# Second-layer router logits: gate matrix as the stationary operand on four column groups, parts added by a 0/1 matrix

## The chip, the cores and the metric

One NeuronCore of one Trainium2 chip runs the whole program. The metric is device time in microseconds (us), from the start to the end of one execution. The profile shows the engines of the core: TensorE (PE for its products, PEld for its weight loads), VectorE (DVE), ScalarE (ACT), GpSimd (POOL) and SyncE (SP, which issues most DMAs).

## The reference, cut to what matters

An attention block gives 2304 rows of 512 numbers. They go through two mixture-of-experts layers with 8 experts each. In both a row goes to the one expert with the largest logit, and the expert's result is scaled by a softmax weight. The change lies in the second layer's router, the line `logits = x @ w_gate`.

```python
def _moe2_ref(x, w_gate, w1, w2):          # x: 2304 x 512, w_gate: 512 x 8
    logits = x @ w_gate
    expert_idx = np.argmax(logits, axis=1)
    logits_shift = logits - logits.max(-1, keepdims=True)
    probs = np.exp(logits_shift)
    probs /= probs.sum(-1, keepdims=True) + 1e-09
    gate_w = probs[np.arange(N), expert_idx]
    out = np.zeros((N, D), dtype=np.float32)
    for e in range(E):
        mask = expert_idx == e
        ...
        xe = x[mask]
        h = np.maximum(xe @ w1[e], 0.0)    # 512 -> 1024
        ye = h @ w2[e]                     # 1024 -> 512
        out[mask] = gate_w[mask, None] * ye
    return out.astype(np.float32)

def reference(**kwargs):
    ...
    x = _moe_ref(x=x, **moe_kwargs)        # first layer
    return _moe2_ref(x=x, **moe2_kwargs)   # second layer
```

## The kernel before

The program has three stretches. Until about 338 us it computes attention and routes the first layer. From there to about 642 us it runs the first layer's experts (L = 0), and after that the second layer's (L = 1). Each layer works in steps of 128 rows that share one expert; `step(L, t)` emits one step.

A step's main work is two products in a split precision: each operand has an upper part (`Wh`, the first of `b.x`, `b.h`) and a lower part (`Wl`, the second of `b.x`, `b.h`), and a product is upper by upper, upper by lower and lower by upper. `s.gemm(0, ph0, ...)` and `s.gemm(0, ph1, ...)` make the two halves of the hidden layer in 12 matmuls each, and `s.gemm(1, py, ...)` makes the result in 24; each matmul streams 512 columns. All are on line L1289.

Around them TensorE transposes in blocks of 128 by 128, four to a call:

- `hT(i, b)` (L1393) transposes half i of the hidden layer, `b.hs[i]`. ScalarE then copies the upper part out of PSUM (`hilo`, L1232), and VectorE subtracts it for the lower part (L1233).
- `xT_pe` (L1228) transposes the gathered rows of the next step into `psx`, again with `hilo` behind it; `next_rows` is both together.
- In the first layer's steps, `yT_pe` (L1334) transposes the last step's result `ysb` into `pm0`, and `yT_ev` (L1337) copies it on ScalarE into `b.hs[0]`, which is free by then.

`logits_pe` (L1330) multiplies this transposed result by the gate matrix `wgT` (128 x 4 x 8, already scaled by -0.5) into `pm1[:, 0:8]`: four float32 products that add up in PSUM, with 128 columns of `b.hs[0]` as weights and 8 columns of `wgT` streaming. `route2` follows on VectorE and ScalarE: minimum (L1350), first index at the minimum (L1351 to L1354, which gives the one-hot `oh`), tanh and the softmax weight (L1356 to L1363). `rank_pe` and `rank_ev` use `oh` two steps later.

The order is written out by hand: an engine does its instructions in the order in which the code emits them. `splits` puts the next expert's weights into upper and lower parts (ScalarE L980, VectorE L983) where an expert changes. The routing of the very last step of layer one is done by `chain1`, a generator that runs beside the second layer's first step; `n1` says how many of its pieces come at each place in that step.

The names: `pm0`, `pm1`, `psx`, `pt0`, `pt1`, `py`, `ph0`, `ph1` are eight PSUM banks of 128 x 512. `pm0` holds nothing but the transposed result in these steps.

Of the kernel before, what the change touches and what calls it, by code (L numbers as in the profile page):

```python
# [8 lines left out]
F32 = mybir.dt.float32  # L9
# [4 lines left out]
ALU = mybir.AluOpType  # L14
# [458 lines left out]
def tile_kernel(ctx, tc, q, k, v, M_prev, z_prev, beta, emb, tau, w1a, w2a, wg, w1b, w2b, out):  # L473
    nc = tc.nc
    B, H, S, D = q.shape
    E, DM, FF = w1a.shape
    NTOK = B * S
    P = 128
    KD, KF = DM // P, FF // P
# [6 lines left out]
    cst = ctx.enter_context(tc.tile_pool(name="cst", bufs=1))  # L486
# [99 lines left out]

    enT = cst.tile([P, KD, E], F32, name="enT")
    wgT = cst.tile([P, KD, E], F32, name="wgT")
    rtau = cst.tile([P, 1], F32, name="rtau")

    def rnorm1(s2, a, hf):
# [17 lines left out]
    def setup_gates(ps_pool, xp):  # L609
        em = xp.tile([E, DM], F32, tag="xb", name="em")  # L610
        sq = rtile([P, 2 * NS * (NS - NE)], "mv", BF16)[0:E, 0:DM]
        sn, sn1 = rtile([E, 1], "sn"), rtile([E, 1], "sn1")

        def load():
            nc.sync.dma_start(out=em, in_=emb)
            nc.sync.dma_start(out=rtau, in_=tau.rearrange("(a b) -> a b", a=1).broadcast_to([P, 1]))
            nc.sync.dma_start(out=wgT, in_=wg.rearrange("(k p) e -> p k e", p=P))

        def squares():
            nc.scalar.activation(out=sq, in_=em, func=AF.Square, accum_out=sn)  # L620
            rnorm1(sn, sn1, half[0:E, 0:1])

        def scale():
            nc.vector.reciprocal(out=rtau, in_=rtau)
            drain(rnorm2(sn, sn, sn1, rtile([E, 1], "sn2")))
            nc.vector.tensor_scalar(out=em, in0=em, scalar1=sn, scalar2=rtau[0:E], op0=ALU.mult, op1=ALU.mult)
            nc.gpsimd.tensor_scalar(out=wgT, in0=wgT, scalar1=-0.5, scalar2=None, op0=ALU.mult)

        def trans():
            ps = setup_gates.ps = ps_pool.tile([P, 512], F32, tag="t", name="psen")  # L630
            for kk in range(KD):
                nc.tensor.transpose(ps[:, E * kk:E * kk + E], em[:, P * kk:P * kk + P], ident[0:E, 0:E])

        def evac():
            nc.vector.tensor_copy(enT.rearrange("p k e -> p (k e)"), setup_gates.ps[:, 0:KD * E])

        return load, squares, scale, trans, evac
# [554 lines left out]
    def rows_of(t):  # L1192

        return xgt[t % 2] if t else xg0
# [19 lines left out]
    psx, pm1, ph1, pt0, pt1, py, pm0, ph0 = (psp.tile([P, 512], F32, name=x) for x in ("psx", "pm1", "ph1", "pt0", "pt1", "py", "pm0", "ph0"))  # L1214
# [11 lines left out]
    def xT_pe(x):  # L1226
        for kk in range(KD):
            nc.tensor.transpose(psx[:, P * kk:P * kk + P], x[:, P * kk:P * kk + P], ident)  # L1228

    def hilo(ps, hl):  # L1230
        hi, lo = hl
        nc.scalar.activation(out=hi, in_=ps, func=AF.Copy)  # L1232
        nc.vector.tensor_tensor(out=lo, in0=ps, in1=hi.bitcast(F32), op=ALU.subtract)  # L1233
# [90 lines left out]
    e2 = []  # L1324
    pts = (pt0, pt1)

    def logits_pe(yT):

        for kk in range(KD):
            nc.tensor.matmul(pm1[:, 0:E], yT[:, P * kk:P * kk + P], wgT[:, kk], start=(kk == 0), stop=(kk == KD - 1))  # L1330

    def yT_pe():
        for kk in range(KD):
            nc.tensor.transpose(pm0[:, P * kk:P * kk + P], ysb[:, P * kk:P * kk + P], ident)  # L1334

    def yT_ev(yT):
        nc.scalar.activation(out=yT, in_=pm0, func=AF.Copy)  # L1337
# [53 lines left out]
    def hT(i, b):  # L1391
        for kk in range(4):
            nc.tensor.transpose(pts[i][:, P * kk:P * kk + P], b.hs[i][:, P * kk:P * kk + P], ident)  # L1393
        hilo(pts[i], b.h[i])

    def next_rows(t):
        xT_pe(rows_of(t))
        hilo(psx, bufs.x)
# [6 lines left out]
    def step(L, t):  # L1405

        s, b = steps[L, t], bufs
        more = 0 < t < NS - 1
        split2 = t > 2
        rt2 = L == 0  # L1410
        late = t >= NT1 - 2
        x = x0 if t == 0 else b.x
        lx = lambda kk: (*x, P * kk)
        lh = lambda kk: (*b.h[kk // 4], P * (kk % 4))
        begin(L, t)
        s.gemm(0, ph0, lx, 0, 0, 3)
        yield
        s.gemm(0, ph0, lx, 0, 3, 9)
        yield
        s.gemm(0, ph0, lx, 0, 9, 12)  # L1420
        if split2:
            s.splits(0, (0, 1))
        nc.scalar.activation(out=b.hs[0], in_=ph0, func=AF.Relu)
        if split2:
            s.splits(1, (0,))

        ahead = (L, t) != (0, NT1 - 1)
        if ahead and split2:
            s.loads(0, (0, 1))
            s.loads(1, (0,))  # L1430
        yield
        s.gemm(0, ph1, lx, 512, 0, 6)
        hT(0, b)
        yield
        rk = L == 0 and 2 <= t <= NT1 - 2
        if rk:
            rank_pe(t - 2)
            rank_ev(t - 2)
        s.gemm(0, ph1, lx, 512, 6, 12)
        last_mm[0] = s.lm[1]  # L1440
        nc.scalar.activation(out=b.hs[1], in_=ph1, func=AF.Relu)
        yield
        if more:
            next_rows(t + 1)
        if rt2:
            yT_pe()
            yT_ev(b.hs[0])
            route2_iov()
        s.gemm(1, py, lh, 0, 0, 3)
        if split2:  # L1450
            s.splits(0, (2,), "h")
        hT(1, b)
        if split2:
            s.splits(0, (2,), "l")
        if more:
            next_step(L, t + 1)
        yield
        s.gemm(1, py, lh, 0, 3, 6)
        cs = (1, 2, 3)
        if t == NE:  # L1460
            s.splits(1, cs)
            cs = ()
        gen = iter(())
        if rt2:
            logits_pe(b.hs[0])
        yield
        s.gemm(1, py, lh, 0, 6, 9)
        if rt2:
            gen = route2(t - 1)
        next(gen, None)  # L1470
        next(gen, None)
        if split2:
            s.splits(0, (3,))
        if split2 and cs:
            s.splits(1, cs)
        if t == 2:
            s.flags()
            s.splits(0, range(4))
            s.loads(0, range(4))
        if not ahead:  # L1480
            e2.append(nc.values_load(ini[0:1, 1, 0:1], engines=[SP_], min_val=0, max_val=E - 1))
            s.loads(0, (0, 1))
            s.loads(1, (0,))
        if split2:
            s.loads(0, (2, 3))
            s.loads(1, (1, 2, 3))
        drain(gen)
        if rk and ((t - 1) % 6 == 0 or t == NT1 - 2):
            c0 = (t - 2) // 6 * 6
            place(c0, t - 1 - c0)  # L1490
        for q_ in range(9, 24, 3):
            yield
            s.gemm(1, py, lh, 0, q_, q_ + 3)
        last_mm[1] = s.lm[1]
        if (L, t) == (1, NT1 - 2):

            nc.gpsimd.drain()
        if rt2:
            nc.gpsimd.dma_start(out=x2[P * (t - 1):P * t, DM:XR], in_=xcb)  # L1499
            if late:  # L1500
                rank_pe(t - 1)
                rank_ev(t - 1)
                place(t - 1, 1)
        if not ahead:

            with tc.If(rg["nt"] <= NT1):
                for c in range(8):
                    for ins in split_chunk(c, rg["wv"]):
                        tc.add_to_no_dep_group("n18", ins)
        end(L, t)  # L1510
# [71 lines left out]
    b = Bufs(lambda i: Wh[0][:, 1, 512 * i:512 * i + 512] if i < 6 else None)  # L1582
# [40 lines left out]
    C = chain0()  # L1623
# [54 lines left out]
    def chain1():  # L1678

        yT_pe()  # L1680
        yT_ev(b.hs[1])
        route2_iov()
        yield
        logits_pe(b.hs[1])
        R = route2(c)
        next(R)
        yield
        next(R)
        yield
        rank_pe(c)  # L1690
        count_pe(pm1[:, 264:264 + E], (c,))
        yield
        next(R)
        rank_ev(c, False)
        yield
        st = {}
        f1 = finish1(1, NS, pm1[:, 264:264 + E], pm1[:, 320:320 + 2 * (NS - NE)], (c,), st)
        for i, x in enumerate(f1):
            next(R, None)
            if i == 3:  # L1700
                drain(R)
                nl = nc.values_load(ini[0:1, 0, 3:4], engines=[SP_], min_val=NT1, max_val=NS)
                nc.sync.dma_start(out=x2[bass.ds((nl - 1) * P, P), DM:XR], in_=xcb)
            yield
            if x == "second":
                second_expert(1)
        gather(1, NE)
        yield
        yield from finish2(1, st)
        fls[1] = st  # L1710

    C, n1 = chain1(), (1, 1, 1, 5, 1, 0, 2, 0, 4, 6, 0)
    s.gemm(0, ph0, lx, 0, 0, 6)
    run(C, n1[0])
    s.gemm(0, ph0, lx, 0, 6, 12)
# [61 lines left out]
```

## Time and profile before

| what | value |
|---|---|
| median of 3 runs | 940.5 us (937.21 to 945.75) |
| the profiled execution | 937.93 us |
| its span, first to last instruction | 936.2 us |
| TensorE products busy | 901.9 us, 96% of the span |
| VectorE, ScalarE, GpSimd busy | 560.7, 525.9 and 278.9 us |

A span is cut by engine: "busy" is time in which an instruction of that engine was under way. Matmuls overlap one another in the pipeline, so the start of one to the start of the next is a better measure of what a matmul costs than its own duration. A group of like instructions in a row is printed as one line with a count.

### The profile page before, as it was taken

The numbers are of one execution on the slowest core, as the hardware profiler recorded it, in microseconds if no ns is written. First come the engines' busy times: TensorE is split into PE (matmuls) and PEld (weight loads), VectorE is DVE, ScalarE is ACT, GpSimd is POOL, SyncE is SP. The second block draws the span as 40 slices with busy tenths as digits, with TensorE's granted clock in tenths as the row PEclk, the third lists the DMA queues.
The fourth block names the chain that finished last, engine by engine and source line by source line (L and its number), as shares of the span: only waits on it lengthen the run. The fifth ranks groups of instructions, "written<-read, shape, count | busy, mean of one in ns | idle before, by whom it ended". The sixth has DMA issues, their size and how long they took to land. (4 is left out here: it accounts for less than half of the span.)

```text
span 936.2 us, 21857 instructions
## 1 busy us (share of the span) xinstructions
PE 901.9 (96%) x5511; PEld 759.0 (81%) x5511; DVE 560.7 (60%) x1825; ACT 525.9 (56%) x1084; POOL 278.9 (30%) x430
## 2 busy tenths in 40 slices
PE   4999999999998999999999999998999999999997
PEld 3888988898887978887788888886868888888885
DVE  4787788787787586548645565543556413473431
ACT  3777868967866754448534563532267424574531
POOL 5555645535542111221221222121112212222221
PEclk9999999999999999999999999999999999999999
DMA  7854748746637116528733405311647613384111
GB/s 159 157 128 90 181 88 238 167 95 136 158 78 241 59 56 224 196 86 279 223 115 102 149 24 168 118 45 39 223 154 266 230 48 119 125 280 161 42 36 38
DMA packets 107562, 129.24 MB, mean 138 GB/s; under 512 B 70906, under 2 KB 70906, under 8 KB 107396
## 3 DMA queue, kind: packets, MB, share of 16 engines
q1 hardware_dynamic: 99364, 104.21, 39.9%
q0 software_dynamic: 8032, 23.22, 7.5%
q8 instruction: 55, 0.90, 0.4%
q14 instruction: 111, 0.91, 0.3%
HBM read 90.32 MB, written 19.25 MB: 117 GB/s over the span
## 5 line engine op out<-in xcount | busy, mean ns | idle before, releaser
L1289 PE MATMUL py<-Wh,b 128*128 (+1 forms) x688 | 243.3, 409 | 2.4 <-DVE b L1233 2.1
L1289 PE MATMUL ph<-Wh,b 128*128 (+1 forms) x672 | 230.5, 403 | 0.9 <-ACTq L1300 0.9
L983 DVE TENSOR_TENSOR Wl<-stg,Wh 128x1024 f32 (+1 forms) x120 | 145.4, 1224 | 87.2 <-ACT Wh L980 74.8
L1289 PEld LDWEIGHTS py<-Wh,b 128*128 128x128 f32 x688 | 129.5, 188 | 30.1 <-DVE b L1233 3.7
L1289 PEld LDWEIGHTS ph<-Wh,b 128*128 128x128 f32 x672 | 126.9, 189 | 30.1 <-ACTq L1300 1.3
L980 ACT ACTIVATE Wh<-stg 128x1024 f32 (+1 forms) x120 | 125.7, 1058 | 24.8 <-DVEq L1300 5.7
L1289 PE MATMUL py<-Wl,b 128*128 (+1 forms) x344 | 135.8, 395 | 0.0
L1289 PE MATMUL ph<-Wl,b 128*128 (+1 forms) x336 | 133.6, 398 | 1.2 <-DVEq L1300 1.2
L1233 DVE TENSOR_TENSOR b<-pt,b 128x512 fp32r<-128x512 f32 x86 | 59.4, 690 | 111.4 <-ACT b L1232 110.3
L355 ACT ACTIVATE att<-psat 128x512 f32<-128x512 f32 (+4 forms) x160 | 69.4, 434 | 59.6 <-PE psat L350 54.2
L370 PE MATMUL psav<-vb,att 128*128 128x128 f32 x640 | 96.0, 281 | 0.5 <-ACT att L355 0.4
L370 PEld LDWEIGHTS psav<-vb,att 128*128 128x128 f32 x640 | 82.7, 191 | 5.9 <-issue 3.8
L1388 POOL DMA_INDIRECT out_dram<-ysb,xca x21 | 26.4, 1258 | 196.4 <-ACTq L1300 126.1
L1232 ACT ACTIVATE b<-pt 128x512 fp32r<-128x512 f32 x86 | 51.5, 598 | 53.7 <-PE pt L1393 40.5
L1383 ACT ACTIVATE ysb<-py,xca 128x512 f32<-128x512 f32 x42 | 28.8, 686 | 87.7 <-PE py L1289 72.4
L337 ACT ACTIVATE a<-a,mx 128x512 f32<-128x512 f32 (+3 forms) x128 | 71.0, 555 | 10.6 <-DVE mx L325 10.3
L325 DVE CUSTOM_DVE_ANT_0 a<-pss,wmask 128x512 f32<-128x512 f32 (+3 forms) x128 | 61.7, 484 | 23.7 <-PE pss L303 23.1
L1289 PEld LDWEIGHTS ph<-Wl,b 128*128 128x128 f32 x336 | 63.7, 190 | 14.9 <-DVEq L1300 1.9
L1289 PEld LDWEIGHTS py<-Wl,b 128*128 128x128 f32 x344 | 65.0, 189 | 10.7
L1198 POOL DMA_INDIRECT xg<-x_scratch,idx x48 | 55.6, 1158 | 38.2 <-POOL xca L1377 10.8
L1499 POOL DMA_DIRECT2D x_scratch<-xcb x21 | 11.9, 565 | 168.9 <-DVE xcb L1363 65.1
L401 POOL TENSOR_TENSOR xb<-tmp,memx 128x256 f32<-128x256 f32 x31 | 22.7, 733 | 125.4 <-DVE tmp L399 125.4
(391 smaller groups left out, 1599.7 us busy)
## 6 DMA issues: line engine op xcount, KB each, us to landing
stg<-in_moe_w_dram SPq DMA_DIRECT2D x120, 512.0 KB
x_scratch<-ysb POOLq DMA_DIRECT2D x22, 256.0 KB, 3.8
L<-L SPq DMA_DIRECT2D x17, 288.0 KB
Hb<-L SPq DMA_DIRECT2D x16, 288.0 KB
H<-H SPq DMA_DIRECT2D x16, 288.0 KB
Hb<-H SPq DMA_DIRECT2D x15, 288.0 KB
qkn<-in_q_dram SPq DMA_DIRECT2D x32, 128.0 KB
qkn<-in_k_dram SPq DMA_DIRECT2D x32, 128.0 KB
```

The lines of the kernel that those rows point to most:

```text
L325: nc.vector.tensor_tensor_reduce(out=av, in0=sv, in1=wv, scale=1.0, scalar=BIG, op0=ALU.add, op1=ALU.min, accum_out=mx[pr],)
L337: nc.scalar.activation(out=a[pr, 0:N], in_=a[pr, 0:N], func=AF.Exp, scale=-1.0, bias=mx[pr], accum_out=rs[pr, c:c + 1])
L355: nc.scalar.activation(out=att[:, 0:N], in_=ps[:, 0:N], func=AF.Copy)
L370: nc.tensor.matmul(ps[:, c], att[:, 128 * kb:128 * kb + 128], vn[:, kb].rearrange("p a d -> p (a d)"), start=(kb == 0), stop=(kb == c))
L980: return nc.scalar.activation(out=chunk(Wh, c, wv), in_=stg[:, c].unsqueeze(1), func=AF.Copy).ins
L983: return nc.vector.tensor_tensor(out=chunk(Wl, c, wv), in0=stg[:, c].unsqueeze(1), in1=chunk(Wh, c, wv).bitcast(F32), op=ALU.subtract).ins
L1198: return nc.gpsimd.indirect_dma_start(out=rows_of(t), out_offset=None, in_=rows, in_offset=bass.IndirectOffsetOnAxis(ap=idx[:, L, t:t + 1] ...
L1232: nc.scalar.activation(out=hi, in_=ps, func=AF.Copy)
L1233: nc.vector.tensor_tensor(out=lo, in0=ps, in1=hi.bitcast(F32), op=ALU.subtract)
L1289: mm = nc.tensor.matmul(ps, x[:, col:col + P], W, start=(first and q_ == qs[0]), stop=(last and q_ == qs[-1]))
L1383: nc.scalar.activation(out=ysb, in_=py, func=AF.Copy, scale=xc[:, 0:1])
L1388: nc.gpsimd.indirect_dma_start(out=out, out_offset=bass.IndirectOffsetOnAxis(ap=xc[:, 1:2].bitcast(I32), axis=0), in_=ysb, in_offset=None, ...
```

## The change

The products of the logits swap sides. The gate matrix, 8 columns for each of the four blocks of 128 inputs, becomes the weights, and the transposed result streams, 128 columns each. Block kk writes partitions 32 kk to 32 kk + 7 of `pm0`, so that each of the four products stands on its own group of 32 columns of the array (`parts_pe`). VectorE copies the 128 x 128 block out (`parts_ev`, over the first 128 columns of `b.hs[0]`, which are no longer needed). A last product with that block as weights and a 128 x 8 matrix `sel` of zeros and ones streaming adds the four parts and turns them into rows by experts (`logits_pe`). `sel` has a one at partition 32 kk + e in column e; the rows of `pm0` between the parts meet zeros.

The transposes of the last result and ScalarE's copy of it move forward, from behind `xT_pe` to right behind `hT(0, b)`. The parts take their old place, ahead of `py`'s first matmuls. VectorE's copy of the parts goes ahead of the lower part of the next rows. In `chain1` there is one more piece, and `n1` is changed by one.

```diff
+    sel = cst.tile([P, E], F32, name="sel")
...
+            nc.gpsimd.memset(sel, 0.0)
+            for kk in range(KD):
+                nc.gpsimd.affine_select(out=sel, in_=sel, pattern=[[-1, E]], compare_op=ALU.not_equal, fill=1.0, base=-32 * kk, channel_multiplier=1)
...
+    def parts_pe(yT):
+        for kk in range(KD):
+            nc.tensor.matmul(pm0[32 * kk:32 * kk + E, 0:P], wgT[:, kk], yT[:, P * kk:P * kk + P], start=True, stop=True)
+
+    def parts_ev(yT):
+        nc.vector.tensor_copy(yT[:, 0:P], pm0[:, 0:P])
+
     def logits_pe(yT):
-        for kk in range(KD):
-            nc.tensor.matmul(pm1[:, 0:E], yT[:, P * kk:P * kk + P], wgT[:, kk], start=(kk == 0), stop=(kk == KD - 1))
+        nc.tensor.matmul(pm1[:, 0:E], yT[:, 0:P], sel, start=True, stop=True)
...
         hT(0, b)
+        if rt2:
+            yT_pe()
+            yT_ev(b.hs[0])
         yield
...
         if more:
-            next_rows(t + 1)
+            xT_pe(rows_of(t + 1))
         if rt2:
-            yT_pe()
-            yT_ev(b.hs[0])
+            parts_pe(b.hs[0])
+            parts_ev(b.hs[0])
+        if more:
+            hilo(psx, b.x)
+        if rt2:
             route2_iov()
...
         route2_iov()
         yield
+        parts_pe(b.hs[1])
+        parts_ev(b.hs[1])
+        yield
         logits_pe(b.hs[1])
...
-    C, n1 = chain1(), (1, 1, 1, 5, 1, 0, 2, 0, 4, 6, 0)
+    C, n1 = chain1(), (1, 1, 1, 6, 1, 0, 2, 0, 4, 6, 0)
```

How this moves instructions is seen best on TensorE in the middle of a first-layer step. Before, from the transposes of the first half of the hidden layer (`hs_5218` is `b.hs[0]`, `pm_5136` is `pm0`, `pm_5131` is `pm1`) to the logits:

```order
L1393 MATMUL pt_5133<-ident,hs_5218 128x128 x4
L1366 LDWEIGHTS tri
...
L1228 MATMUL psx<-ident,xg_5220 128x128 x4
L1334 MATMUL pm_5136<-ident,ysb 128x128 x4
L1289 ISA
L1289 MATMUL py<-Wh_5124,b_5225 128x512
...
L1330 MATMUL pm_5131<-wgT,hs_5218 128x8
L1300 UNCONDITIONAL_BRANCH
L1330 MATMUL pm_5131<-wgT,hs_5218 128x8 x3
```

Now, at the same place (here `hs_5232` is `b.hs[0]`, `pm_5150` is `pm0`, `pm_5145` is `pm1`):

```order
L1406 MATMUL pt_5147<-ident,hs_5232 128x128 x4
L1347 MATMUL pm_5150<-ident,ysb 128x128 x4
L1379 LDWEIGHTS tri
...
L1233 MATMUL psx<-ident,xg_5234 128x128 x4
L1336 MATMUL pm_5150<-hs_5232,wgT 8x128 x4
L1294 ISA
L1294 MATMUL py<-Wh_5138,b_5239 128x512
...
L1343 MATMUL pm_5145<-sel,hs_5232 128x8
```

The four transposes of `ysb` have moved forward past half of a hidden-layer product, the four parts (8 x 128 results) stand where they stood, and one product is left at the place of the logits.

The other place is VectorE in the second layer's first step, where `chain1` routes the last rows. Before (`t8s`, `km_5145` and `oh` are the route's; `b_5226` is the lower part of the transposed hidden half):

```order
L1343 TENSOR_SCALAR iov<-ioer,xcb 128x8
L1350 TENSOR_REDUCE mn<-pm_5131 128x1
L1351 SCALAR_TENSOR_TENSOR t8s<-pm_5131,mn,iov 128x8
L1353 TENSOR_REDUCE km_5145<-t8s 128x1
L1354 TENSOR_SCALAR oh<-t8s,km_5145,xcb 128x8
L1233 TENSOR_TENSOR b_5226<-pt_5133,b_5225 128x512
L1370 SCALAR_TENSOR_TENSOR rj,rkb<-pm_5131,oh 128x8
```

Now (`b_5240` is that lower part):

```order
L1356 TENSOR_SCALAR iov<-ioer,xcb 128x8
L1339 COPY hs_5233<-pm_5150 128x128
L1363 TENSOR_REDUCE mn<-pm_5145 128x1
L1364 SCALAR_TENSOR_TENSOR t8s<-pm_5145,mn,iov 128x8
L1238 TENSOR_TENSOR b_5240<-pt_5147,b_5239 128x512
L1366 TENSOR_REDUCE km_5159<-t8s 128x1
L1367 TENSOR_SCALAR oh<-t8s,km_5159,xcb 128x8
L1383 SCALAR_TENSOR_TENSOR rj,rkb<-pm_5145,oh 128x8
```

The copy of the parts is new, and the two instructions that make `oh` have fallen behind the lower part of the hidden half.

## Rows read from the trace of the kernel before

**Rows 1.** The page's busy times: engine, busy us, share of the span, instructions

```profile
PE 901.9 (96%) x5511; PEld 759.0 (81%) x5511; DVE 560.7 (60%) x1825; ACT 525.9 (56%) x1084; POOL 278.9 (30%) x430
```

**Rows 2.** Busy times in the first layer's stretch; PEclk is the granted clock

```profile
338.00:642.00 304.00, 300.10 (x1613) 247.41 (x1611) 180.29 (x599) 147.60 (x228) 59.15 (x111) 1.00 0.42 136
```

**Rows 3.** What TensorE waited for in that stretch: us, times, longest

```profile
PE py L1289 <- DVE b L1233: 2.1, 2, 1.1
```

**Rows 4.** Timeline of TensorE: the logits of two steps, seven steps apart

```profile
466.28 0.95 PE L1330 MATMUL pm<-wgT,hs 128*128 128x8 f32 x8
...
563.93 0.95 PE L1330 MATMUL pm<-wgT,hs 128*128 128x8 f32 x8
```

**Rows 5.** Groups by form on TensorE: the logits' products

```profile
L1330 PE MATMUL pm<-wgT,hs 128*128 128x8 f32 x176 | 21.0, 245 | 0.0
```

**Rows 6.** Timeline of TensorE in one step: start us, us, operation

```profile
477.54 0.60 PE L1228 MATMUL psx<-ident,xg 128*128 128x128 f32 x4
477.97 0.60 PE L1334 MATMUL pm<-ident,ysb 128*128 128x128 f32 x4
...
480.23 0.95 PE L1330 MATMUL pm<-wgT,hs 128*128 128x8 f32 x8
481.04 0.48 PE L1289 MATMUL py<-Wh,b 128*128 x1
481.36 0.40 PE L1289 MATMUL py<-Wl,b 128*128 x1
481.59 0.63 PE L1289 MATMUL py<-Wh,b 128*128 x2
```

**Rows 7.** Timeline of TensorE in attention, where 64 columns stand between 128

```profile
171.76 0.83 PE L229 MATMUL psm<-mz,pht 128*128 128x130 f32 x6
172.43 1.05 PE L370 MATMUL psav<-vb,att 128*128 128x128 f32 x8
...
173.89 0.38 PE L229 MATMUL psm<-mz,pht 128*128 128x130 f32 x2
174.20 0.43 PE L231 MATMUL psm<-mz,pht 128*64 128x130 f32 x2
174.57 0.94 PE L370 MATMUL psav<-vb,att 128*128 128x128 f32 x6
175.34 0.38 PE L350 MATMUL psat<-ident,a 128*128 128x128 f32 x2
```

**Rows 8.** Timeline of TensorE in attention, ten passes of 64 columns by 64

```profile
103.09 0.80 PE L376 MATMUL psav<-vb,att 128*64 128x64 f32 x10
103.82 0.55 PE L350 MATMUL psat<-ident,a 128*128 128x128 f32 x3
```

**Rows 9.** Timeline of ScalarE in the step of rows 6

```profile
477.73 0.60 ACT L1441 ACTIVATE hs<-ph 128x512 f32<-128x512 f32 x1 [0.94 <-PE ph L1289]
...
478.70 0.61 ACT L1337 ACTIVATE hs<-pm 128x512 f32<-128x512 f32 x1
```

**Rows 10.** Timeline of VectorE in that step

```profile
478.85 0.69 DVE L1233 TENSOR_TENSOR b<-psx,b 128x512 fp32r<-128x512 f32 x1 [1.18 <-ACT b L1232]
```

**Rows 11.** Groups by form on VectorE: a copy out of PSUM

```profile
L220 DVE COPY pht<-pspr 128x64 f32<-128x64 f32 x16 | 3.4, 214 | 0.2
```

**Rows 12.** Groups by form, and timeline, of GpSimd

```profile
L550 POOL TENSOR_SCALAR_AFFINE_SELECT pw<-pw 128x2 f32<-128x2 f32 x12 | 2.3, 189 | 0.5
...
51.95 0.72 POOL L401 TENSOR_TENSOR xb<-tmp,memx 128x256 f32<-128x256 f32 x1 [2.64 <-DVE tmp L399]
```

**Rows 13.** Timeline of VectorE in the second layer's first step

```profile
650.98 0.29 DVE L1354 TENSOR_SCALAR oh<-t8s,km,xcb 128x8 bf16<-128x8 f32 x1
652.81 0.69 DVE L1233 TENSOR_TENSOR b<-pt,b 128x512 fp32r<-128x512 f32 x1 [1.55 <-ACT b L1232]
```

**Rows 14.** Timeline of TensorE in the same place

```profile
653.39 0.18 PE L1366 MATMUL pm<-oh,tri 128*128 128x8 bf16 x1
```

## The prediction

> **What bounds the kernel now.** I read the page first: TensorE has a product under way in 96% of the span, and no other engine is over 60% [rows 1]. So time comes from TensorE, unless something makes it wait. The logits that the change touches lie in the first layer's stretch, so the stretch is read next: in 304 us TensorE is busy for 300, at a granted clock of 1.00, which is the 2.4 GHz level, while VectorE has 180 and ScalarE 148 [rows 2]. Then the waits of that stretch: besides one of 0.3 us, TensorE waits only twice for another engine, 2.1 us in total, each time for the lower part of the hidden half, which comes late because VectorE is busy with a new expert's weights [rows 3]. Last the rhythm: the logits of two steps that are seven apart begin at 466.28 and 563.93 [rows 4], 13.95 us a step. TensorE is issued back to back here. A nanosecond that the change takes from its stream or adds to it shows in the end, and work on the other engines shows only if it makes TensorE wait.
>
> **The products that go.** The group has 176 passes [rows 5], for 22 routings of four products, so a float32 product is two passes. In a step the eight begin at 480.23, and the next matmul at 481.04; the one after comes 0.32 us later, where the usual distance is 0.23 (481.36 to 481.59) [rows 6]. Together 0.81 + 0.09 = 0.90 us for eight passes, 0.112 each. A pass here streams only 8 columns, so it is the load of its 128 weight columns that takes the time.
>
> **The products that come.** The parts have the sides swapped: 8 weight columns and 128 streaming ones. What does a float32 pass cost when its weights are few? Attention has one place: two passes with 64 weight columns and 130 streaming ones run from 174.20 to 174.57 [rows 7], and ten passes with 64 and 64 from 103.09 to 103.82 [rows 8]. If a place costs a fixed amount and each pass a time in proportion to its streamed columns, the two equations (2 passes of 130 in 0.37, 10 of 64 in 0.73) give 0.061 us for 64 columns, 0.12 for 130 and 0.12 to 0.13 of fixed cost. So a pass with 128 streaming columns costs about 0.11 however few weights it has. That is what an old pass costs, and there are again eight. The swap by itself gains nothing; what it can gain is that the four groups run side by side.
>
> The fixed cost is the second thing to see. Six passes with 128 weight columns go from 171.76 to 172.43, 0.112 each. Where two passes with 64 weight columns stand among such, the ten passes from 173.89 to 175.34 take 1.45 us, not 1.12 [rows 7]: 0.33 more for going to the narrower column size and back. It falls on both sides: 0.31 from the first of the two wide ones to the narrow ones (two usual passes are 0.22), and 0.77 for the six behind them (usual 0.67). Some 0.05 of it is the uncovered load of 64 weight columns, less with 8. I take 0.30 for the parts' way in and out of four groups of 32; no row has groups of 32, so the bounds are 0 and 0.33.
>
> The Trainium skill, "TensorEngine Tiling (Array Packing)", section "Key Properties", says the same as a rule: changing the tiling mode, and not just the tile, drains TensorE. It speaks against this change, since the parts change the mode twice in every step; no figure of it is used.
>
> How far the eight passes overlap no row shows. Bounds: not at all, 8 x 0.11 = 0.88; or all four groups at once, two passes behind each other, 2 x 0.11 and a little for the issue of eight, 0.25. I take the middle way: instructions start in order, the second pass of a group needs its own columns free and so waits for the first, but the first pass of the next group can start beside it. That is five slots of 0.11, 0.55.
>
> The product with `sel` has 128 weight columns and 8 streaming, two passes like the old ones: 2 x 0.112 = 0.22.
>
> Sum for a step: 0.55 + 0.30 + 0.22 = 1.07, against 0.90 before: **0.17 us slower**.
>
> **What moves.** The four transposes of `ysb` cost 0.44 with their neighbours (477.54 to 477.97 is one such four) [rows 6]; moved behind four other transposes they cost the same. ScalarE's copy of them (0.61) goes ahead of the relu of the second half, where ScalarE sits idle for 0.94 us [rows 9]; it is done before the parts ask for it, about a microsecond after the transposes. If that cover were gone, the relu would come up to 0.6 late and TensorE would wait in the next `hT`; in the steps with a new expert ScalarE has caught up by then too, so I count nothing.
>
> **VectorE's copy** of 128 x 128 out of PSUM: a 128 x 64 copy takes 0.21 [rows 11], a 128 x 512 subtraction 0.69 [rows 10], so about 0.28. It is queued ahead of the lower part of the next rows, where VectorE waits 1.18 us for ScalarE [rows 10]; the parts end within that idle time. Behind it in the queue are the next rows' lower part, which is needed a whole phase later, and the hidden half's lower part, needed some 12 matmuls (2.8 us) on. The logits ask for the copy six matmuls and four transposes after the parts. Nothing to add. GpSimd's fill of `sel` is a memset and four selects of 0.19 each, under 1 us once, into an idle time of 2.64 [rows 12]: nothing.
>
> **The two late steps.** In the two steps where TensorE waits 1.0 and 1.1 us for VectorE [rows 3], 0.17 more of TensorE's own work shortens the wait by as much. So 20 of 22 routings pay.
>
> **The second layer's first step.** There `oh` was ready at 651.3, and `rank_pe` took it at 653.39 [rows 13, 14]. Now the logits come six matmuls later (1.4 us) and `oh` is made behind the lower part of the hidden half, which starts at 652.81 and takes 0.69 [rows 13]. With the stream some 0.3 us later that is 653.8, and `oh` is done at about 654.3, while TensorE comes to `rank_pe` at about 653.7: a wait of 0.6 us, once.
>
> **The sum**: 20 x 0.17 + 0.6 = 4.0 us. On the profiled execution that is 937.9 + 4.0 = 941.9. That execution was among the faster of the three runs; I place the forecast on their median, 940.5 + 4.0 = **944.5 us**. The runs of one kernel here spread by 0.9%, so about 1% is what a measurement can tell from no change.
>
> **Rivals.**
>
> *The groups don't run side by side* (so the change doesn't do what its words say): eight slots, 0.88 + 0.30 + 0.22 = 1.40, 0.50 more a step. 20 x 0.50 + 0.6 = 10.6 us, 951.1, slower. For it: float32 passes come in pairs on the same columns, and no row shows two products at once. Against it: the narrow passes of rows 8 do follow each other at once, so nothing else slows them. It decides from where more than five of the eight slots are in series; at seven the loss is near 8 us.
>
> *All groups at once*: 0.25 + 0.30 + 0.22 = 0.77, 0.13 less a step. In the late steps the gain is lost to the wait, so 20 x 0.13 - 0.6 = 2.0 us, 938.5.
>
> *All at once and no cost for the column size*: 0.25 + 0.22 = 0.47, 0.43 less a step, 20 x 0.43 - 0.6 = 8.0 us, 932.5. Against it stand the 0.33 us of rows 7. The Trainium skill, same page, section "When to Use Tiling", advises just this swap where the streaming side is 32 columns or fewer, with four column groups; taken by its word, up to four times as fast, it would be this rival. No run so far shows it.
>
> **How the numbers follow.** Five slots: 0.42, within 1% but for a small tail. In series: 0.33; its 951.1 is 1.1% up, so two thirds of it lie over 1%. All at once: 0.17, within 1%. All at once and free: 0.08, near -0.9%, a part of it over 1%. That gives faster 0.06, same 0.68, slower 0.26. The range takes in the second and the third case, with the spread of the median: 936 to 953; what is left out is mainly the free case.
>
> **What would show it.** In the profile after, the distance of two steps' logits: 14.1 us by my sum, 14.45 in series, 13.8 all at once. In a step, from the last transpose of `psx` to the first matmul of `py`: some 0.85 us for the parts. The starts of their eight passes tell the overlap: pairs that begin together, or 0.11 apart throughout. TensorE's waits in the first layer stay at two for VectorE, and one new wait of about 0.6 us for `oh` stands in the second layer's first step. I would be wrong if the parts wait for ScalarE's copy in many steps, or if VectorE's copy makes the logits late: then a wait of `pm` for `hs` appears in every step, which I count at nothing.

## The result, and the profile after

| | before | after |
|---|---|---|
| median of 4 runs, us | 940.57 (937.21 to 945.75) | 931.38 (929.1 to 932.39) |
| the profiled execution, us | 937.93 | 932.39 |

The ratio is 0.9894, with a 95% interval of 0.9844 to 0.9944. The change made the kernel some 9 us faster. That is below the predicted range, and on the other side of the time before.

The page's busy times of the changed kernel, to be held against [rows 1]:

```profile
PE 893.2 (96%) x5555; PEld 748.4 (80%) x5555; DVE 566.5 (61%) x1847; ACT 526.3 (57%) x1084; POOL 280.1 (30%) x435
```

TensorE has 44 instructions more than before and is busy for 8.7 us less. That is the first sign that something beside the logits became cheaper: 22 routings can't give back 8.7 us out of [rows 5] unless each loses 0.40 of its 0.90.

The rhythm, as [rows 4] had it: the parts of two steps, seven steps apart, on TensorE's timeline after.

```profile
465.62 0.41 PE L1336 MATMUL pm<-hs,wgT 128*8 128x128 f32 x8
...
561.00 0.41 PE L1336 MATMUL pm<-hs,wgT 128*8 128x128 f32 x8
```

That is 95.38 us, 13.63 a step, against 13.95 before: 0.32 less. Over 20 steps it is 6.5 us, so the first layer's steps alone don't give 9. The second layer is the next place to look, and there the change touches nothing but the first step. Two transposes of gathered rows, one step apart, on TensorE's timeline of the kernel before:

```profile
834.64 0.60 PE L1228 MATMUL psx<-ident,xg 128*128 128x128 f32 x4
...
847.14 0.60 PE L1228 MATMUL psx<-ident,xg 128*128 128x128 f32 x4
```

and of the changed kernel:

```profile
830.20 0.60 PE L1233 MATMUL psx<-ident,xg 128*128 128x128 f32 x4
...
842.50 0.60 PE L1233 MATMUL psx<-ident,xg 128*128 128x128 f32 x4
```

The step takes 12.30 instead of 12.50 us, with the same instructions in the same order. Inside it every matmul of the expert products (512 columns) has become a little shorter. Ten matmuls before, first and last:

```profile
723.98 0.39 PE L1289 MATMUL py<-Wl,b 128*128 x1
...
726.07 0.40 PE L1289 MATMUL py<-Wl,b 128*128 x1
```

and after:

```profile
723.48 0.39 PE L1294 MATMUL py<-Wl,b 128*128 x1
...
725.52 0.39 PE L1294 MATMUL py<-Wl,b 128*128 x1
```

Nine distances are 2.09 us before and 2.04 after, 232 and 227 ns each; the granted clock is 1.00 in both stretches. Over all of both layers the mean distance of two such matmuls in a row is 233 ns before and 228 after, in the first layer as in the second. Of the durations that the page prints, 0.39 and 0.40, nobody would see it; the starts show it. A step has 48 such matmuls, so 5 ns each are the 0.2 us of a step, and 44 steps make some 9 us.

Now the middle of a step after, for [rows 6]:

```profile
478.70 0.60 PE L1233 MATMUL psx<-ident,xg 128*128 128x128 f32 x4
479.23 0.41 PE L1336 MATMUL pm<-hs,wgT 128*8 128x128 f32 x8
479.56 0.50 PE L1294 MATMUL py<-Wh,b 128*128 x1
479.90 0.39 PE L1294 MATMUL py<-Wl,b 128*128 x1
480.13 0.40 PE L1294 MATMUL py<-Wh,b 128*128 x1
480.36 0.60 PE L1406 MATMUL pt<-ident,hs 128*128 128x128 f32 x4
480.72 0.48 PE L1294 MATMUL py<-Wh,b 128*128 x1
481.04 0.40 PE L1294 MATMUL py<-Wl,b 128*128 x1
481.27 0.39 PE L1294 MATMUL py<-Wh,b 128*128 x1
481.50 0.28 PE L1343 MATMUL pm<-sel,hs 128*128 128x8 f32 x2
481.64 0.48 PE L1294 MATMUL py<-Wh,b 128*128 x1
481.96 0.40 PE L1294 MATMUL py<-Wl,b 128*128 x1
```

Four transposes between matmuls, counted to the second matmul behind them, are 480.36 to 481.04, 0.68. With the parts between, the same is 478.70 to 479.90, 1.20. The parts so cost **0.52**. The product with `sel` is 481.50 to 481.96, 0.46 where the usual distance is 0.23: **0.23**. Together 0.75, where the old logits cost 0.90.

How the eight passes overlap is seen with the stretch cut into tenths of a microsecond. The windows view of the parts' line alone (us, TensorE's products with their count, weight loads with their count):

```profile
479.20:479.30 0.10, 0.07 (x4) 0.08 (x8) 1.00 0.05 20
479.30:479.40 0.10, 0.10 (x8) 0.04 (x8) 1.00 0.10 41
```

In the first tenth four passes are under way, in the second all eight. From their single records, the distances from one start to the next are 7, 7, 6, 94, 6, 7 and 6 ns: four passes together, then four together. The Trainium skill, "TensorE: Matmul & The Clock Gate", section "Part 3: Packing small matmuls — row/col tiling", says that products on different groups of the array start some 4 ns apart. This trace has 6 to 7.

The way in and out is there as well: the last transpose of `psx` is followed by the first part after 0.20 us instead of 0.11, the last part by the first matmul of `py` after another 0.20. The Trainium skill, "TensorEngine Tiling (Array Packing)", section "Key Properties", says that a change of the tiling mode drains TensorE; the 0.20 on both sides agree.

VectorE's copy of the parts in that step, in its idle time [rows 10], and the place in the second layer's first step that [rows 13, 14] showed before, on VectorE:

```profile
479.77 0.29 DVE L1339 COPY hs<-pm 128x128 f32<-128x128 f32 x1 [1.35 <-PE pm L1336]
...
650.29 0.69 DVE L1238 TENSOR_TENSOR b<-pt,b 128x512 fp32r<-128x512 f32 x1 [0.69 <-ACT b L1237]
...
651.08 0.29 DVE L1367 TENSOR_SCALAR oh<-t8s,km,xcb 128x8 bf16<-128x8 f32 x1
```

`oh` now stands behind the lower part, and TensorE waits for it. This wait and the others of the first layer's stretch, on TensorE's timeline:

```profile
388.15 0.50 PE L1294 MATMUL ph<-Wl,b 128*128 x1 [0.74 <-DVEq L1305]
...
451.23 0.50 PE L1294 MATMUL py<-Wh,b 128*128 x1 [1.50 <-DVE b L1238]
...
568.86 0.17 PE L749 MATMUL pm<-acc,ones 128*128 128x8 bf16 x1 [0.24 <-DVE acc L1385]
...
587.55 0.66 PE L1406 MATMUL pt<-ident,hs 128*128 128x128 f32 x4 [0.29 <-ACTq L1305]
...
651.42 0.17 PE L1379 MATMUL pm<-oh,tri 128*128 128x8 bf16 x1 [0.42 <-DVE oh L1367]
```

The two waits for VectorE's lower part [rows 3] are still there and are 2.4 us together; four small ones have come, 1.7 us. One more loss follows the longest wait. The windows view around it (the third number from a row's end is the granted clock):

```profile
440.00:452.00 12.00, 10.50 (x62) 8.23 (x61) 11.20 (x25) 8.54 (x13) 1.48 (x4) 0.99 0.84 284
452.00:456.00 4.00, 4.00 (x14) 3.29 (x14) 2.95 (x9) 1.93 (x3) 1.01 (x1) 0.60 0.80 265
456.00:460.00 4.00, 4.00 (x20) 3.30 (x19) 2.00 (x7) 0.69 (x1) 0.56 (x1) 1.00 0.73 247
```

After the wait of 1.50 the granted clock is 0.60 in the next 4 us, for the most part the 1.2 GHz level, and matmuls stand 427 ns apart; that step takes 16.96 us, against 15.36 before, where the wait was 1.12 and the granted clock stayed at 1.00.

### The profile page after: what moved, and what is told of

Read it like the earlier page. It is cut to its first block, busy times and chain, and to the rows that moved or that the text cites. A ratio compares the mean times of both kernels' runs of the same rounds, so it can differ in the third digit from the quotient of the medians.

```text
span 930.7 us, 21977 instructions
## 1 busy us (share of the span) xinstructions
PE 893.2 (96%) x5555; PEld 748.4 (80%) x5555; DVE 566.5 (61%) x1847; ACT 526.3 (57%) x1084; POOL 280.1 (30%) x435
## 5 line engine op out<-in xcount | busy, mean ns | idle before, releaser
L1294 PE MATMUL ph<-Wh,b 128*128 (+1 forms) x672 | 227.9, 400 | 1.0 <-ACTq L1305 0.9
L1294 PE MATMUL ph<-Wl,b 128*128 (+1 forms) x336 | 131.7, 392 | 2.0 <-DVEq L1305 2.0
```

The lines of the kernel that those rows point to most:

```text
L1294: mm = nc.tensor.matmul(ps, x[:, col:col + P], W, start=(first and q_ == qs[0]), stop=(last and q_ == qs[-1]))
```

## The experiments

The result left two questions. **Why do matmuls that the change doesn't touch run at 228 ns and not 233?** My theory was the place in memory. `sel` takes 32 bytes of each partition among the constants, and every tile allocated behind it begins 32 bytes later, the weights `Wh` and `Wl` among them: in the memory map of the built program the first one begins at byte 69,312 of a partition before and at 69,344 after. The tiles `b`, which are loaded into the array while `Wh` or `Wl` stream, are in another pool and stay at 217,056 and every 2,048 bytes behind. Modulo 64 that is 0 (`Wh` and `Wl`, which stream) against 32 (`b`) before, and 32 against 32 after. The rival: the new order of instructions, or the new form of the logits, makes TensorE's stream denser. **And what is the change itself worth?** Here the theory was that the four groups run at once and give 0.13 to 0.15 us a step back; the rival, that the groups give nothing and the gain is all from elsewhere. The first four experiments stand beside a median of the kernel before of 940.97, the last four beside one of 939.84, each of 25 runs. Two distances are read in each trace: that of a first-layer step (seven steps, as above) and that of a second-layer step.

**The kernel before, with an unused tile where `sel` would be.** Streaming operand at 32, `b` at 32 modulo 64.

```diff
     wgT = cst.tile([P, KD, E], F32, name="wgT")
+    pad = cst.tile([P, E], F32, name="pad")
```

> The kernel before with an unused tile of 32 bytes a partition at the place where the change puts sel; the instructions are the same, and the expert weights Wh and Wl lie 32 bytes higher. Theory A (most of the gain is the new address of the weights, not the new products): the distance of two expert matmuls falls from 233 to 227 or 228 ns in both layers, a first-layer step from 13.95 to 13.75 us, a second-layer step from 12.49 to 12.29, and the time by 8 to 9 us, to about 932. Rival B (the new order or the products set the distance): 233 ns as before, time within 2 us of the kernel before.

933.16 us, ratio 0.9924 (0.9896 to 0.9952). No instruction differs from the kernel before. The second layer's step, on TensorE's timeline:

```profile
829.84 0.60 PE L1229 MATMUL psx<-ident,xg 128*128 128x128 f32 x4
...
842.15 0.60 PE L1229 MATMUL psx<-ident,xg 128*128 128x128 f32 x4
```

12.31 us, as in the changed kernel. The first layer's, seven steps apart:

```profile
465.57 0.95 PE L1331 MATMUL pm<-wgT,hs 128*128 128x8 f32 x8
...
562.03 0.95 PE L1331 MATMUL pm<-wgT,hs 128*128 128x8 f32 x8
```

That is 13.78 a step; the distance of matmuls is 228 ns. So 32 bytes of memory that nobody reads or writes are worth 7.8 us.

**The changed kernel, with `Wh` and `Wl` put back to where they were.** Two one-column constants become one tile, which makes room for `sel`.

```diff
-    k1, ntl = ctile([P, 1], "k1"), ctile([P, 1], "ntl")
+    kn = ctile([P, 2], "kn")
+    k1, ntl = kn[:, 0:1], kn[:, 1:2]
```

> The changed kernel with two tiles of one number each (k1 and ntl) put into one, so that sel takes the freed 32 bytes and the expert weights lie where they lay before. Theory A: distance of two expert matmuls back at 233 ns, a second-layer step at 12.49 us, a first-layer step at 13.80 (13.95 less 0.15 for the products), time about 937 to 940. Rival B: 227 ns, steps of 13.61 and 12.29, time about 931.

937.53 us, ratio 0.9963 (0.9938 to 0.9987); its steps:

```profile
828.45 0.60 PE L1234 MATMUL psx<-ident,xg 128*128 128x128 f32 x4
...
840.95 0.60 PE L1234 MATMUL psx<-ident,xg 128*128 128x128 f32 x4
```

12.50 us, as before the change, 233 ns from matmul to matmul, and 13.82 in the first layer. The profiled execution took 944.93, the longest of the twelve, but both distances lie where the granted clock is 1.00. With the address effect taken out, the change gains 3.4 us, 0.13 in a step.

**Shift the other side.** The kernel before, with an unused tile of 32 bytes in the pool that holds `b`, so that `b` moves and `Wh` and `Wl` stay: 0 against 0.

```diff
+    fp.tile([P, 8], F32, name="pad")
```

> The kernel before with an unused tile of 32 bytes behind the x, h and result buffers, which puts all of them 32 bytes lower, and with them the operands that are loaded as weights of the array; Wh and Wl, which stream, stay. Theory A1 (what counts is how the two operands lie to one another, modulo 64 bytes): now both lie at a multiple of 64, so 227 ns and about 932 us. Theory A2 (the address of the streaming operand alone counts): 233 ns and about 940 us.

932.75 us, ratio 0.9913 (0.9885 to 0.9942); 228 ns, steps of 13.77 and 12.31, the second from these lines:

```profile
827.75 0.60 PE L1228 MATMUL psx<-ident,xg 128*128 128x128 f32 x4
...
840.06 0.60 PE L1228 MATMUL psx<-ident,xg 128*128 128x128 f32 x4
```

Moving the other operand by the same amount does the same. So it isn't the place of `Wh` and `Wl` that counts, but how the two operands stand to each other.

**The changed kernel with the same line added:** 32 against 0.

> The changed kernel with the same 32 bytes behind the x, h and result buffers: Wh and Wl stay 32 above a multiple of 64, the x, h buffers come to a multiple of 64. Theory A1: the operands lie 32 bytes apart modulo 64 again, 233 ns, steps of 13.80 and 12.49 us, about 939 us. Theory A2: 227 ns, as the changed kernel, about 931 us.

936.07 us, ratio 0.9958 (0.9937 to 0.9979); 233 ns, steps of 13.81 and 12.51:

```profile
831.98 0.60 PE L1233 MATMUL psx<-ident,xg 128*128 128x128 f32 x4
...
844.49 0.60 PE L1233 MATMUL psx<-ident,xg 128*128 128x128 f32 x4
```

The changed kernel is slowed by the very line that makes the kernel before faster. This crossing rules out that the order of instructions or the logits made the matmuls shorter.

**Equal modulo 64, but 64 apart modulo 128.** The kernel before with an unused tile of 96 bytes.

```diff
+    pad = cst.tile([P, 3 * E], F32, name="pad")
```

> The kernel before with an unused tile of 96 bytes in place of 32: the weights' addresses and those of the x, h buffers are then equal modulo 64, but 64 apart modulo 128. Theory A (64 bytes is the period): 227 ns, a second-layer step of 12.29 us, 932 to 933 us. Rival B (they must be equal modulo 128): 233 ns and 12.49 us, 940 us.

934.61 us, ratio 0.994 (0.9909 to 0.9972). Its second-layer step:

```profile
830.28 0.60 PE L1229 MATMUL psx<-ident,xg 128*128 128x128 f32 x4
...
842.63 0.60 PE L1229 MATMUL psx<-ident,xg 128*128 128x128 f32 x4
```

12.35, with matmuls 229.6 ns apart: neither 228 nor 233. Most of the effect goes by the difference modulo 64, and some 1.6 ns are left that it doesn't explain.

**All four products on one group.** The changed kernel, with the four products added up in PSUM on the first group of 32, as many passes as before, and `sel` reduced to its first block.

```diff
-            for kk in range(KD):
+            for kk in range(1):
                 nc.gpsimd.affine_select(out=sel, ...)
...
-            nc.tensor.matmul(pm0[32 * kk:32 * kk + E, 0:P], wgT[:, kk], yT[:, P * kk:P * kk + P], start=True, stop=True)
+            nc.tensor.matmul(pm0[0:E, 0:P], wgT[:, kk], yT[:, P * kk:P * kk + P], start=(kk == 0), stop=(kk == KD - 1))
```

> The changed kernel with its four products on one column group: they add up in partitions 0 to 7 of pm0, and sel has ones in its first eight rows only; everything else, and every address, is as in the changed kernel. Theory A (the four groups stream at once, and that is the gain of the products): the eight passes come 0.11 us apart, the parts take 1.2 us in place of 0.53, a first-layer step is 0.6 to 0.7 us longer (13.61 to about 14.25) and the time 12 to 14 us longer, 944. Rival B (the groups matter little, a narrow pass is short by itself): step within 0.1 us of 13.61, time 931.

943.45 us, ratio 1.0039 (1.0018 to 1.006), and on TensorE's timeline:

```profile
481.85 0.60 PE L1233 MATMUL psx<-ident,xg 128*128 128x128 f32 x4
482.38 1.04 PE L1336 MATMUL pm<-hs,wgT 128*8 128x128 f32 x8
483.35 0.51 PE L1294 MATMUL py<-Wh,b 128*128 x1
483.69 0.40 PE L1294 MATMUL py<-Wl,b 128*128 x1
```

The parts now take 0.97 from the first to the next matmul, where the changed kernel takes 0.33; the passes start 109 to 113 ns apart. A step is 14.28. The records don't name a pass's group, but here, on the same columns, they start about 109 ns apart; so the four that start within 20 ns in the changed kernel are on four groups, one pass of each. The way in and out is as dear as with four groups (0.53 from the first transpose to the first part in both), so it belongs to the narrow column size and not to the use of several groups. What the four groups give by running side by side is 0.64 a step. Without it the changed kernel takes 943.45 instead of 931.38, and even the shorter matmuls (228 ns here too) don't make up for the swap.

**The move alone.** The kernel before with the 32 bytes of the first experiment, and the transposes of `ysb` and ScalarE's copy moved to their new place; the old logits.

```diff
         hT(0, b)
+        if rt2:
+            yT_pe()
+            yT_ev(b.hs[0])
...
             next_rows(t + 1)
         if rt2:
-            yT_pe()
-            yT_ev(b.hs[0])
             route2_iov()
```

> The kernel before with the unused 32 bytes, and of the change the move alone: the transposes of the last result and their copy stand right behind hT(0), the logits are the four old products. Theory A (the move is free, the products save 0.15 to 0.17 us a step): first-layer step of 13.78 us as with the 32 bytes alone, 933 us. Rival B (the move is what saves): 13.61 us, 931 us.

933.36 us, ratio 0.9943 (0.9917 to 0.9969), steps of 13.81 and 12.30. Beside the first experiment's 933.16, 13.78 and 12.31, the move costs next to nothing: six of the seven steps take 13.76 or 13.77, one 14.08.

**The late steps, tried again.** The changed kernel with VectorE's and ScalarE's weight splits put in another order around `hT`: upper parts where they were, lower parts and the next loads behind `hT(0)`; and `n1` one piece earlier, so that `oh` is made ahead of the lower part.

```diff
-            s.splits(0, (0, 1))
+            s.splits(0, (0, 1), "h")
...
-            s.splits(1, (0,))
+            s.splits(1, (0,), "h")
...
+        if split2:
+            s.splits(0, (0, 1), "l")
+            s.splits(1, (0,), "l")
...
-    C, n1 = chain1(), (1, 1, 1, 6, 1, 0, 2, 0, 4, 6, 0)
+    C, n1 = chain1(), (1, 1, 2, 5, 1, 0, 2, 0, 4, 6, 0)
```

> The changed kernel with two waits taken out by order: the lower parts of the next expert's first chunks are emitted behind hT(0), with the loads that reuse their stage, and in the second layer's first step oh is made ahead of the hidden half's lower part. Theory A (TensorE's waits for VectorE, 0.9 and 1.5 us, and the stretch at half clock behind the second are due to VectorE's queue): these waits go, steps 8 to 10 take 13.6 to 14 us, the wait of 0.42 for oh goes, time 927 to 929. Rival B (the wait moves to the weights' lower parts or to the loads that start later): waits of equal size before other matmuls, 931 or more.

932.76 us, ratio 0.9924 (0.9897 to 0.9951), not better than the changed kernel. TensorE's waits, from the end of attention to 690 us (us in total, times, longest):

```profile
PE pm L1343 <- DVE hs L1339: 1.7, 3, 0.7
PE pt L1406 <- ACTq L1305: 1.4, 1, 1.4
PE psx L1233 <- DMA xg<-x_scratch,idx: 1.0, 1, 1.0
```

The two waits for the lower part and the one for `oh` are gone, but the product with `sel` now waits three times for VectorE's copy of the parts, the transposes wait 1.4 for ScalarE, and gathered rows come late once. The wait at 388 is still there, with 0.67 for 0.74. The granted clock no longer falls in these steps. The steps with a new expert lose about as much as before, only at other places. Whether some order of these splits is free of waits is left open.

## Why the prediction was wrong

**The step that failed outright** is "A nanosecond that the change takes from its stream or adds to it shows in the end", as I used it: the sum then counts the instructions that the change adds and removes, and takes all others for unchanged in cost. `sel` was counted only as an engine's work ("GpSimd's fill of `sel` ... nothing"), not as 32 bytes that move other tiles. They changed the cost of some 2,000 matmuls by 5 ns. The first experiment shows this part alone at -7.8 us, the third at -8.2 by the other operand; it is nearly all of the measured -9.2. No rival had it. That the fast rival's 932.5 lies near the result is chance: its mechanism, no cost for the column size, is not what happened.

**The term that was mis-sized** is "five slots of 0.11, 0.55" for the parts' overlap. The trace shows two slots: all four first passes, then all four second passes. This is the rival "all groups at once", which I gave 0.17: parts with the way in and out 0.25 + 0.30 = 0.55, measured 0.52. I had reasoned that the second pass of a group holds up the groups behind it; the starts show, together with the one-group kernel, that the first passes of all four come ahead of the second ones. A step so gains 0.15 at equal matmuls (13.78 in the first experiment, 13.63 after; 13.95 before, 13.82 and 13.81 in the second and fourth), where I forecast a loss of 0.17 and the rival a gain of 0.13.

**What held.** A float32 product stays two passes, and eight in series take what the series rival said: 0.88 + 0.30 = 1.18 a step. In the one-group kernel the stretch from the first transpose to the second matmul is 1.84 (481.85 to 483.69), less the 0.68 without parts 1.16. Its time, 951.1, would by my estimate stand if matmuls had kept 233 ns: 943.45 + 7.8 = 951.3. The two equations gave 0.12 for a pass of 128 columns and I went on with 0.11; the one-group kernel has 0.109. The profiled execution, 937.93, was not one of the three runs, as I had put it, but a fourth; the sum doesn't use that. The way in and out of the narrow column size was sized rightly from [rows 7], and the product with `sel` at 0.22 (0.23). The move is free. VectorE's copy, estimated at 0.28, takes 0.29 and lies in idle time in the ordinary step. The wait for `oh` came, 0.42 where I had 0.6.

**The late steps** were half right. I took it that in two steps the gain or loss would vanish in the wait [rows 3]. The two waits go with the step, though only roughly: 2.1 before, 2.5 in the first experiment and 2.4 after, where steps are shorter, 2.3 and 2.0 in the second and fourth, and 1.3 in the one-group kernel with its steps of 14.28. But three small ones came that I hadn't foreseen: 0.74, 0.24 and 0.29. They stand, at 0.15 to 1.02 us each, in the profiles of the kernels with the parts (the last one not in that with the new order of splits) and in none of the kernels with the old logits, the one with the move included. Waits of 0.15 us or more between 338 and 660 us, without those at the change of layers, sum to 4.6 us after and 2.9 in the first experiment. So of 20 x 0.15 = 3.0 gained, 1.7 goes to waits and 1.3 is left; the medians, 933.16 and 931.38, say 1.8, though the intervals of the two ratios overlap. The stretch at the lower clock, 1.6 us in the profiled execution, is not in this sum, and no profile shows how many of the other executions had it. Where the addresses are as before the change, its own part is seen by itself: 3.4 us (ratio 0.9963) and, with the other operand shifted, 4.9 (0.9958), both intervals below 1.

Added up from my forecast: +4.0, less 20 x (0.17 + 0.15) = 6.4 for the overlap, less 8 for the addresses, and 1 or 2 for the waits that I hadn't counted, gives -8.4 to -9.4. Measured was -9.2.

**What stays open.** Why a matmul takes 5 ns longer when its two operands differ by 32 bytes modulo 64 was not tested; the runs show only that it goes by the difference and not by either address, and that 64 bytes of difference cost a little too. What starts the wait at 388.15 is open too: VectorE's split of that weight, which waits for ScalarE's upper part, begins at 383.68, in the first experiment at 382.60, and what makes ScalarE later isn't shown.

## What to carry to other kernels

Where TensorE bounds the kernel, a new tile is an edit of its own: look in the memory map at what moves behind it, and before believing a gain or a loss, run the old kernel with an unused tile of the same size. Read the distance of matmuls that the change doesn't touch in both traces; if it differs, the change has done something that its diff doesn't say. Small products on separate groups of columns do run side by side, but the way in and out and the product that adds the parts eat most of that: here 0.64 us of overlap left 0.15.

## What the runs showed of the hardware that I had not expected

- The distance of 512-column products in a row was 233 ns where the streaming operand (`Wh`, `Wl`) and the one loaded into the array (`b`) differed by 32 bytes modulo 64 (the kernel before, the second and the fourth experiment), 228 where they were equal (after, and the other experiments but one), and 229.6 where they were equal modulo 64 and 64 apart modulo 128.
- Four float32 products on four column groups start as four first passes 6 to 7 ns apart, then, 94 ns behind the last of these, four second passes; not product by product.
- Going from 128 weight columns to 8 and back takes 0.20 us from pass to pass on either side instead of 0.11, with one group in use as with four.
- A single wait of 1.50 us was followed by a granted clock of 0.60 over 4 us, and so was one of 1.58 in the second experiment (0.59); in the same place waits of 1.03 to 1.40 in the other kernels were not (1.00). The step took 1.6 us longer.
